# Linear attention and a ResMLP block on one core: two copies of q moved to ScalarE, weight loads moved up in GpSimd's queue, and a new order of all later work

## The chip, the cores and the metric

The kernel runs on one core of a Trainium2 chip. The core has five engines with a queue each: TensorE (PE; its weight loads are shown apart as PEld), VectorE (DVE), ScalarE (ACT), GpSimd (POOL) and SyncE (SP). Each works through its own list in order and waits on semaphores for the others. The metric is the device time of one execution in microseconds (us), lower is better.

## The reference

Attention without a softmax, then a norm, then two residual blocks. The inputs q, k and v are [8, 8, 576, 64] (batch, heads, sequence, width of a head); x is laid out as [8, 576, 512].

```
kv  = einsum('bhsd,bhse->bhde', k, v)
out = einsum('bhsd,bhde->bhse', q, kv)
x   = out / sqrt(mean(out*out, -1) + 1e-6) * g_norm      # per head, then heads side by side
a1  = alpha1 * x + beta1
u   = x + lam * einsum('ts,bsd->btd', w_tok, a1)          # mixes the 576 tokens
a2  = alpha2 * u + beta2
y   = u + lam * (relu(a2 @ w_ch1) @ w_ch2)                # 512 -> 2048 -> 512
```

## The kernel before, in words

One batch is one round of work. Its 576 rows are cut into four chunks of 128 and a tail of 64; the tails of two batches share one tile, so most tail work happens once per two batches. A batch goes through these steps, with the lines that the profile shows:

- Loads: k and v by GpSimd (load_kv, L1395 for 512 rows, L1399 for the tail), q by SyncE (load_q, L1387, four loads a batch). GpSimd also loads both weights of the channel mix in four pieces each (load_w1 L1372, load_w2 L1378). In the trace both are named in_moe_w_ch_dram.
- Attention: kᵀv on PE (L634, tails L640), copied out by ACT (L651) and DVE (L653, tile kvc). q is transposed, for the first two batches on PE (qt_early: copies into a padded tile at L583 or L586, transposes L590, copies out L600 and L603), later by DVE and ACT (L1405, L1408).
- Norm: q·kv on PE (L725), square on ACT (L692), sum on DVE (L695), root on ACT (L698), reciprocal and products on DVE (L701, L703, L710), and the product for the token mix on GpSimd (L713, tile rm; for the tails DVE L708, tile rtl). The first batch has its own form of it (norm_half, L751 to L787).
- Token mix: PE L808, tails L853; the sum is added by DVE (L818). GpSimd turns the result to bf16 (L896) and SyncE transposes it by DMA (L909, tiles a2m, and a2l for the tails).
- Channel mix: first layer on PE (L1020, tails L1034), relu on ACT (L913, tails L1042 or L1051); second layer on PE (L1081) for the first two batches, with the sums added by L1257 and L1266. From the third batch on, the second layer is done by Strassen's scheme with seven products in place of eight: sums of blocks on DVE (L1104), products on PE (L1142), kept sums through ACT (L1172) and GpSimd (L1175), last sums on DVE (L1180). For the last two batches the first layer is done the same way over the pair (L961, evicted by ACT L973 and DVE L983, relu L987 or L913).
- Folds: after the second batch, alpha2 is multiplied into the first weight (fold_w1, L1062, DVE) and lam into the second (fold_w2, L1071).
- The result goes out by SyncE (L1271, L1276, L1193, L1189).

What sets the order: all steps are first recorded as numbered operations with what they read and write. The table ORDER then lists these numbers in the order in which they are issued: each engine's list is that order cut down to its own operations. A number followed by a colon gives the PSUM banks of what it writes, two numbers with a plus are two groups of matmuls woven one by one, and ~n stands for n spare matmuls that keep PE busy (L461). GATES adds a few dependences. Semaphores are worked out from the order afterwards. So an operation that waits holds up everything behind it in its engine's list, and nothing else sets priorities. ORDER's numbers and banks have no meaning by themselves; what they do is shown below as rows of each engine.

The first batches' q copies, with the condition that the change edits:

```
dst, src = qi[b][j][:, :, 64 * m:64 * m + 64], (q0s, q1s)[b][:, at[m]]
if m and not b:
    P.op("ACT", act(576), lambda e, ...: e.activation(dst, src, ACT.Identity), ...)
else:
    P.op("POOL", pool(576, 0), lambda e, ...: e.tensor_copy(out=dst, in_=src), ...)
```

Of the kernel before, what the change touches and what calls it, by code (L numbers as in the profile page):

```python
# [24 lines left out]
13 0 3 6 30 4 31 ~32 14 7 1 32 12 9 28 5 8 207 10 11 27 21 36 35 20 34 29 19 48 42:1 47 ~5 18 26  # L25
16 49:2 25 15 17 2 51:4 55:5:6 50 ~3 56 52 43 23 53:3 44:7 57 61 58 22 62 59 63 54 60 64 126:1 45
72:4:5 37 127 65:2:3 73 41 128 79:6 311 312 74 66 189 136:1:7 24 188 80 67 75 190 76 137 81 68 191
129 69 77 39 82 38 ~2 70 134:5 78 142 130:4 138 135 143 139 132:2 144 83 140 84 131 86:5 87 ~3 145
# [1522 lines left out]
```

## Time and profile before

| what | value |
|---|---|
| median of three runs | 334.18 us (333.53 to 335.07) |
| the profiled execution | 333.56 us |
| its span, first to last instruction | 331.7 us |
| granted TensorE clock | 1.000 |
| matmuls | 2457 |
| PE busy | 321.7 us, 97% |
| DVE busy | 250.8 us, 76% |
| ACT busy | 175.7 us, 53% |
| POOL busy | 150.2 us, 45% |

The span leaves out 1.86 us before the first and behind the last instruction. Times in rows are counted from the span's start. A row of the timeline gives the start, the busy time, the engine, the line, the operation, its output and inputs, and the number of instructions of that kind in a row; in brackets stands how long the engine stood idle before it and what ended that. Matmuls overlap, so the distance between starts says more about PE's pace than the length of one.

### The profile page before, as it was taken

The page shows a single profiled execution, that of the slowest core. Times are in us where ns is not written, and L with a number is a line of the kernel's source. Part 1 is how long each engine was busy: PE and PEld are TensorE (multiplying, and loading weights), DVE is VectorE, ACT ScalarE, POOL GpSimd, SP SyncE. Part 2 cuts the span into 40 slices and gives each one's busy share as a digit, 9 for nine tenths or more (in the row PEclk, how much of TensorE's full clock was granted, in tenths as well). Part 3 has the DMA queues.
Part 4 walks back from the last instruction along what each step waited for, and adds up shares of the span by engine and source line. Part 5 has one row for each costly group of instructions (what it writes and reads, how often), then busy time and mean ns, then how long its engine had stood idle before and what let it go on. Part 6 is the DMA issues. An engine that isn't in the chain of part 4 may idle for free.

```text
span 331.7 us, 6183 instructions
## 1 busy us (share of the span) xinstructions
PE 321.7 (97%) x2457; PEld 218.7 (66%) x2457; DVE 250.8 (76%) x443; ACT 175.7 (53%) x361; POOL 150.2 (45%) x149
## 2 busy tenths in 40 slices
PE   6999899999999999999999999999999999999996
PEld 6777564464676445786579874787568575458884
DVE  3596068669799998939984498769889786989633
ACT  5664573329634482619842676731794059872011
POOL 3599119799253643443357044554325610003432
PEclk9999999999999999999999999999999999999999
DMA  7999999999943996499049942597400170000134
GB/s 243 323 253 230 213 230 201 203 165 275 214 140 79 179 245 116 77 320 192 17 65 268 245 75 50 87 300 163 103 0 3 30 177 0 3 0 2 63 125 130
DMA packets 108532, 48.15 MB, mean 145 GB/s; under 512 B 82061, under 2 KB 101717, under 8 KB 108504
## 3 DMA queue, kind: packets, MB, share of 16 engines
q1 hardware_dynamic: 81520, 26.24, 33.7%
q0 software_dynamic: 26800, 21.38, 33.1%
q8 instruction: 19, 0.31, 0.4%
q10 hardware_dynamic: 184, 0.14, 0.2%
q14 instruction: 9, 0.07, 0.1%
HBM read 38.82 MB, written 9.44 MB: 145 GB/s over the span
## 4 chain that ended last, share of the span: by engine, by line
PE 69%; DVE 14%; POOL 7%; DMA 6%; issue 2%; ACT 2%; SPq 1%; DVEq 0%; POOLq 0%
PE ps L1020 20%; PE ps L1142 18%; PE ps L808 8%; PE ps L961 7%; PE ps L1081 6%; PE ps L1034 3%; DVE small L695 2%; DMA w<-in_moe_w_ch_dram 2%; DVE ps L703 2%; DMA a2l<-a2b 2%; DMA w<-in_k_dram 2%; PE ps L634 2%; DVE xm L710 2%; PE ps L725 2%; POOL rm L713 1%
## 5 line engine op out<-in xcount | busy, mean ns | idle before, releaser
L1020 PE MATMUL ps<-a2m,w 128*128 128x512 bf16 x384 | 98.2, 384 | 1.4 <-DMA w<-in_moe_w_ch_dram 0.8
L713 POOL TENSOR_TENSOR rm<-xm,la_bc 128x512 bf16<-128x512 f32 x28 | 37.2, 1331 | 61.4 <-DVE xm L710 61.2
L1020 PEld LDWEIGHTS ps<-a2m,w 128*128 128x128 bf16 x384 | 36.2, 97 | 39.5 <-issue 1.5
L913 ACT ACTIVATE hh<-ps,b 128x512 bf16<-128x512 f32 x72 | 48.8, 685 | 15.9 <-PE ps L1020 14.8
L1175 POOL TENSOR_TENSOR xm<-xm,tmp 128x512 f32<-128x512 f32 x18 | 25.2, 1411 | 55.1 <-ACT tmp L1172 55.1
L725 PE MATMUL ps<-kvc,qt 128*128 128x128 f32 (+1 forms) x140 | 42.2, 404 | 0.0
L1142 PE MATMUL ps<-w,hh 128*128 128x256 bf16 x344 | 40.5, 273 | 0.1
L1081 PE MATMUL ps<-w,hh 128*128 128x512 bf16 x144 | 37.7, 385 | 0.0
L1142 PEld LDWEIGHTS ps<-w,hh 128*128 128x128 bf16 x344 | 33.5, 98 | 5.9 <-issue 0.4
L634 PE MATMUL ps<-vr,kr 128*128 128x128 f32 x112 | 34.8, 409 | 0.0
L695 DVE TENSOR_REDUCE small<-sq 128x8 f32<-128x512 f32 (+1 forms) x35 | 23.5, 679 | 13.8 <-ACT sq L692 13.4
L1180 DVE TENSOR_TENSOR xm<-ps,xm 128x512 f32<-128x512 f32 x24 | 16.4, 685 | 20.6 <-POOL xm L1175 14.4
L808 PE MATMUL ps<-rm,wt 128*128 128x512 bf16 x112 | 30.2, 382 | 1.0 <-DVE rtl L708 0.4
L1172 ACT ACTIVATE tmp<-ps 128x512 f32<-128x512 f32 (+1 forms) x21 | 11.9, 566 | 33.8 <-PE ps L1142 33.8
L896 POOL CAST a2b<-xm 128x512 bf16<-128x512 f32 x24 | 15.9, 665 | 29.5 <-DVE xm L818 29.4
L692 ACT ACTIVATE sq<-ps 128x512 f32<-128x512 f32 (+1 forms) x35 | 20.6, 595 | 15.9 <-PE ps L725 15.7
L725 PEld LDWEIGHTS ps<-kvc,qt 128*128 128x128 f32 (+1 forms) x140 | 27.2, 195 | 2.1 <-DVE kvc L653 0.8
L703 DVE TENSOR_TENSOR ps<-ps,small 128x512 f32<-128x512 f32 (+1 forms) x35 | 24.2, 693 | 0.5
L913 ACT ACTIVATE hh<-ps 128x512 bf16<-128x512 f32 x32 | 17.6, 597 | 12.4 <-PE ps L1020 12.3
L634 PEld LDWEIGHTS ps<-vr,kr 128*128 128x128 f32 x112 | 22.4, 200 | 1.7
L1081 PEld LDWEIGHTS ps<-w,hh 128*128 128x128 bf16 x144 | 13.3, 97 | 13.6 <-issue 0.4
L1408 ACT ACTIVATE qt<-qp 128x576 fp32r<-128x576 f32 x24 | 16.2, 682 | 8.2 <-DVE qp L1405 8.1
(197 smaller groups left out, 616.8 us busy)
## 6 DMA issues: line engine op xcount, KB each, us to landing
out_dram<-xm SPq DMA_DIRECT2D x32, 256.0 KB, 2.7
kr<-in_k_dram POOLq DMA_DIRECT2D x7, 1024.0 KB, 6.5
vr<-in_v_dram POOLq DMA_DIRECT2D x7, 1024.0 KB, 7.9
qs<-in_q_dram SPq DMA_DIRECT2D x24, 288.0 KB, 4.7
w<-in_moe_w_ch_dram POOLq DMA_DIRECT2D x8, 512.0 KB, 9.9
xm<-in_q_dram SPq DMA_DIRECT2D x8, 288.0 KB, 5.5
qs<-in_v_dram SPq DMA_DIRECT2D x4, 288.0 KB, 6.2
w<-in_k_dram SPq DMA_DIRECT2D x4, 288.0 KB, 6.3
```

Of the source, the lines that this page charges most:

```text
L634: P.mm("fill", 128, [lambda e, t=t, c=c, h=h, o=128 * (h % 4): e.matmul(t.ap()[:, o:o + 128], kr4[:, h, c:c + 2, :].rearrange("p c d -> p ...
L695: P.op("DVE", dve(n), lambda e: e.tensor_reduce(out=st, in_=sq[rs, s3, 0:nst, :], axis=AX.X, op=ALU.add), r=[("sq", s3)], w=[("sm", s4)])
L703: P.op("DVE", dve(n), lambda e: e.tensor_tensor(out=grp(ps()), in0=grp(ps()), in1=st[..., None].to_broadcast([rs.stop - rs.start, nst, DH] ...
L713: P.op("POOL", pool(n), lambda e: e.tensor_tensor(out=r, in0=x.rearrange("p h e -> p (h e)"), in1=la, op=ALU.mult), r=xks + ["la"], w=rks)
L725: P.mm("fill", 128, [lambda e, p=p: e.matmul(dst(p), qt[:, p, cs], kvc[:, i, p, :], start=(p == 0), stop=(p == 3)) for p in range(4)], r=[ ...
L808: P.mm("fill", 512, [lambda e, sc=sc: e.matmul(t.ap(), wt[:, sc if sc < 4 else tw(b), 128 * c:128 * c + 128], rsrc(b, sc, al), start=(sc = ...
L913: P.op("ACT", act(512, 0 if f is None else 1), lambda e: e.activation(dst, t.ap(), ACT.Relu, bias=0.0 if f is None else b1[:, f:f + 1]), r ...
L961: P.mm("main", 512, [lambda e, i=i: e.matmul(t.ap(), lhs[:, i, 128 * x + o:128 * x + o + 128], rhs[:, i, :], start=(first and i == 0), sto ...
L1020: P.mm("main", 512, [lambda e, dj=dj: e.matmul(t.ap(), w1[:, dj, 128 * fj:128 * fj + 128], a2m[:, b % 2, dj, :], start=(dj == 0), stop=(dj ...
L1081: P.mm("main", 512, [lambda e, fj=fj, t=t, c=c: e.matmul(t.ap(), (ht[:, fj, 128 * c:128 * c + 128] if c < 4 else hl[:, fj, :]), w2[:, fj, ...
L1142: P.mm("main", 256, [lambda e, c=c, fj=fj: e.matmul(t.ap()[:, 256 * c:256 * c + 256], at[:, fj, 128 * c:128 * c + 128], rhs(fj), start=(fi ...
L1175: P.op("POOL", pool(256 * n), lambda e, cs=cs, f=f: e.tensor_tensor(out=X[:, cs, f], in0=X[:, cs, f], in1=two(tmp[:, s]), op=ALU.add), r=x ...
```

## The change

The condition in qt_early for the second batch is widened, and the table ORDER is replaced. No operation is added or taken away, the matmuls and the spare ones are the same, and GATES is the same.

```diff
@@ ORDER @@
-13 0 3 6 30 4 31 ~32 14 7 1 32 12 9 28 5 8 207 10 11 27 21 36 35 20 34 29 19 48 42:1 47 ~5 18 26
-16 49:2 25 15 17 2 51:4 55:5:6 50 ~3 56 52 43 23 53:3 44:7 57 61 58 22 62 59 63 54 60 64 126:1 45
...
+47 16 15 17 49:2 2 51:4 50 55:5:6 52 ~3 43 23 56 53:3 22 57 44:7 61 58 62 59 63 60 54 64 45 126:1
+72:4:5 127 65:2:3 37 73 79:6 311 312 74 66 136:1:7 128 41 80 67 75 137 189 24 76 68 81 188 ~2 129
...
@@ qt_early @@
             for m in range(2):
                 dst, src = qi[b][j][:, :, 64 * m:64 * m + 64], (q0s, q1s)[b][:, at[m]]
-                if m and not b:
+                if m == j if b else m:
                     P.op("ACT", act(576), lambda e, dst=dst, src=src: e.activation(
                         dst, src, ACT.Identity), r=[("st", key, at[m])], w=[("qi", b, j, m)])
                 else:
```

For the second batch (b = 1) each of the two steps j has two copies m; the one with m equal to j now runs on ACT at L583, the other stays on GpSimd at L586. PE's list is the same up to about 53 us, so ahead of that only the lists of the other engines differ.

The first place is GpSimd's list at about 22 us, where the second batch's copies of q (qp and xm), its loads of v (vr) and k (kr) and the pieces of the weights (w1, w2) stand. L787 is the first batch's product for the token mix.

```order
-L586 COPY qp<-xm 128x9x64 x2
-L586 COPY xm<-xm 128x9x64
+L586 COPY qp<-xm 128x9x64
 L1395 DMA vr<-in_v_dram 128x8x256
+L1372 DMA w1<-in_moe_w_ch1_dram 128x4x512
 L787 TENSOR_TENSOR rm<-xm,la_bc 128x2x256 x2
 L787 TENSOR_TENSOR rtl<-xt,la_bc 64x256
-L1372 DMA w1<-in_moe_w_ch1_dram 128x4x512 x2
+L1372 DMA w1<-in_moe_w_ch1_dram 128x4x512
```

Two copies have left the list ahead of v's load, and the second piece of w1 stands right behind that load instead of behind three products. Further down, the fourth quarter of w2 moves up behind the third in the same way, from behind the first L713.

The second place is DVE's list at about 213 us, in the Strassen step of the fifth batch. hh and hs are the hidden values and their sums, xm the rows of the result. Before:

```order
L1104 TENSOR_TENSOR hh<-hh 128x4x256
L710 TENSOR_TENSOR xm<-ps,g_bc 128x512
L1104 TENSOR_TENSOR hs<-hh 128x1024
L1180 TENSOR_TENSOR xm<-ps,xm 128x2x256
L1104 TENSOR_TENSOR hh<-hh,hs 128x4x256
L1104 TENSOR_TENSOR hh<-hs,hh 128x4x256
L1104 TENSOR_TENSOR hh<-hh,hs 128x4x256
L1104 TENSOR_TENSOR hh<-hs,hh 128x4x256
L695 TENSOR_REDUCE small<-sq 128x8 x2
```

And after:

```order
L1104 TENSOR_TENSOR hh<-hh 128x4x256
L710 TENSOR_TENSOR xm<-ps,g_bc 128x512
L1104 TENSOR_TENSOR hs<-hh 128x1024
L1104 TENSOR_TENSOR hh<-hs,hh 128x4x256
L1104 TENSOR_TENSOR hh<-hh,hs 128x4x256
L1104 TENSOR_TENSOR hh<-hs,hh 128x4x256
L695 TENSOR_REDUCE small<-sq 64x8
L1104 TENSOR_TENSOR hh<-hh,hs 128x4x256
L695 TENSOR_REDUCE small<-sq 128x8
L701 RECIPROCAL small<-small 64x8
L695 TENSOR_REDUCE small<-sq 128x8
L1180 TENSOR_TENSOR xm<-ps,xm 128x2x256
```

The four sums that read both hh and hs stood behind the L1180 and stand ahead of it now, with a reduction of the seventh batch's norm between them. PE's list at that place changes with them: before, 36 L1034 of the tails (20 and 16, with eight products between) stood ahead of the first product with ab_bc and hh, and now it is 12 L1034 and four L1020, with 12 L1034 behind the products.

The third place is PE's list at about 267 us, where the channel mix of the last two batches begins: w and a2l are the first weight and the tails' input to it.

```order
 L1142 MATMUL ps<-w,hh 128x256 x16
-L1142 MATMUL ps<-ws,hh 128x256 x16
+L1142 MATMUL ps<-ws,hh 128x256 x8
+L1034 MATMUL ps<-a2l,w 128x128 x4
+L1142 MATMUL ps<-ws,hh 128x256 x8
+L1034 MATMUL ps<-a2l,w 128x128 x36
+L961 MATMUL ps<-a2m,w 128x512 x4
 L1034 MATMUL ps<-a2l,w 128x128 x20
-L961 MATMUL ps<-a2m,w 128x512 x4
-L1034 MATMUL ps<-a2l,w 128x128 x24
 L961 MATMUL ps<-qp,qs 128x512 x4
```

Forty L1034 stand ahead of the first L961 where 20 stood before. Behind this, the L961 of the pair stage and the tails still to come are interleaved in another way. At about 55 us PE has 16 L1081 ahead of the token mix of the second batch where it had 12, and 16 behind its tails where it had 20.

More of the change, by code (lines that the diff above doesn't have):

```diff
@@ L24 @@
 ORDER = """
-13 0 3 6 30 4 31 ~32 14 7 1 32 12 9 28 5 8 207 10 11 27 21 36 35 20 34 29 19 48 42:1 47 ~5 18 26
-16 49:2 25 15 17 2 51:4 55:5:6 50 ~3 56 52 43 23 53:3 44:7 57 61 58 22 62 59 63 54 60 64 126:1 45
-72:4:5 37 127 65:2:3 73 41 128 79:6 311 312 74 66 189 136:1:7 24 188 80 67 75 190 76 137 81 68 191
-129 69 77 39 82 38 ~2 70 134:5 78 142 130:4 138 135 143 139 132:2 144 83 140 84 131 86:5 87 ~3 145
[75 rows of a table removed]
+13 3 6 0 4 30 7 14 ~32 31 9 12 1 32 8 28 5 10 207 11 27 21 48 35 20 36 34 19 26 29 18 42:1 25 ~5
+47 16 15 17 49:2 2 51:4 50 55:5:6 52 ~3 43 23 56 53:3 22 57 44:7 61 58 62 59 63 60 54 64 45 126:1
+72:4:5 127 65:2:3 37 73 79:6 311 312 74 66 136:1:7 128 41 80 67 75 137 189 24 76 68 81 188 ~2 129
+69 77 190 82 191 142 70 138 134:5 78 130:4 39 135 143 132:2 139 38 144 83 140 84 131 86:5 87 ~3
[75 rows of a table added]
 """
```

150 rows, old and new, of the table ORDER are left out of this document.

## The prediction

> **What bounds the kernel now.** I read the busy shares first, then the chain that ended last, then what TensorE waited for.
>
> ```profile
> span 331.7 us, 6183 instructions
> PE 321.7 (97%) x2457; PEld 218.7 (66%) x2457; DVE 250.8 (76%) x443; ACT 175.7 (53%) x361; POOL 150.2 (45%) x149
> PE 69%; DVE 14%; POOL 7%; DMA 6%; issue 2%; ACT 2%; SPq 1%; DVEq 0%; POOLq 0%
> ```
>
> TensorE (PE) is busy for 321.7 of 331.7 us, so a new order of the same matmuls can only win from the 10.0 us in which it stands still. The second view lists its waits by what ended them:
>
> ```profile
> PE ps L1020 <- DMA w<-in_moe_w_ch_dram: 0.8, 1, 0.8
> PE ps L1020 <- DVE w L1062: 0.6, 1, 0.6
> PE ps L1142 <- DVE hh L1104: 0.6, 1, 0.6
> PE ps L1034 <- DMA a2l<-a2b: 0.4, 1, 0.4
> PE ps L808 <- DVE rtl L708: 0.4, 1, 0.4
> ```
>
> Each occurs once. Since PE's list is one serial chain, a wait removed there shortens the span by as much, unless a later wait grows. A wait costs more than its idle time, because a matmul's modelled end lies behind the start of the next. I therefore price each by the distance between starts less the usual distance.
>
> **The front: w1's second piece.** POOL's and PE's rows (start, busy us, instruction, and in brackets the idle time and what ended it):
>
> ```profile
> 22.74 0.66 POOL L586 COPY xm<-xm 128x576 f32<-128x576 f32 x1
> 23.35 0.95 POOL L1395 DMA_DIRECT2D vr<-in_v_dram  x1
> 24.32 2.52 POOL L787 TENSOR_TENSOR rm<-xm,la_bc 128x512 bf16<-128x512 f32 x2
> ...
> 27.47 1.56 POOL L1372 DMA_DIRECT2D w<-in_moe_w_ch_dram  x2
> 33.83 0.41 PE L634 MATMUL ps<-vr,kr 128*128 128x128 f32 x1
> 35.08 0.38 PE L1020 MATMUL ps<-a2m,w 128*128 128x512 bf16 x1 [0.84 <-DMA w<-in_moe_w_ch_dram]
> 35.11 0.41 PE L634 MATMUL ps<-vr,kr 128*128 128x128 f32 x1
> 35.36 0.39 PE L1020 MATMUL ps<-a2m,w 128*128 128x512 bf16 x1
> DMA to landing us min/median/max: 7.5/8.6/10.5
> ```
>
> The last line is of L1372's four loads. The piece issued at 27.47 landed 7.5 us later, at 34.97, and L1020 went at 35.08. From an L634 to the next L1020 it is 35.36 − 35.11 = 0.25, so it could have gone at 34.08: 1.00 us is lost. The change takes two copies out ahead of v's load; copies follow each other at 23.35 − 22.74 = 0.61, so v is issued 1.22 earlier, at 22.13, and the piece right behind it at 22.13 + 0.95 = 23.08, which is 4.39 us sooner. If the queue of loads itself were the limit (v's megabyte stands before it in both orders), nothing is gained; if the latency of 7.5 counts, it lands at 30.6 and the whole 1.00 goes. It has to land only 0.9 us sooner for that, a fifth of the lead. I take **0.8**, with bounds 0 and 1.0. The L787s behind it are pushed by one issue (1.56 / 2 = 0.78) and pulled by 1.22, so they come no later. The fourth quarter of w2 moves ahead of an L713 of the second batch: one more issue of 0.78 there, hidden by the L1081 rows that PE runs before the L808 which reads that product (the one that PE met late near 55 us was DVE's, below); were it not hidden it would cost 0.78. So I set it at nothing.
>
> The trace sits on the careful side of a rule here. "DMA: Bandwidth & Descriptors" of the Trainium skill (Anatomy of one DMA) fits a GpSimd load as 2.0 us plus its bytes over 436 GB/s, which for a 512 KB piece gives an estimate of 3.2 us, less than half of the 7.5 seen; by it the wait would go whole, and the sum would be 0.2 larger.
>
> The two copies land on ACT:
>
> ```profile
> 14.92 0.67 ACT L583 ACTIVATE tmp<-xm 128x576 f32<-128x576 f32 x1
> 22.09 0.30 ACT L779 ACTIVATE small<-small,eps 128x8 f32<-128x8 f32 x1
> 25.13 1.51 ACT L603 ACTIVATE qt<-ps 128x512 fp32r<-128x512 f32 x3 [2.74 <-PE ps L590]
> ```
>
> Two times 0.67 is 1.34 us, from 22.39 to 23.73, within the 2.74 us that ACT stood idle: nothing. Without that cover they would cost 1.34.
>
> **Matmuls put ahead of a wait.** In three places the new order has PE do other work while the late operand arrives.
>
> ```profile
> 53.83 1.67 PE L1081 MATMUL ps<-w,hh 128*128 128x512 bf16 x7
> 55.91 1.04 PE L808 MATMUL ps<-rm,wt 128*128 128x512 bf16 x4 [0.40 <-DVE rtl L708]
> 55.16 0.69 DVE L708 TENSOR_TENSOR rtl<-ps,e_bc 64x512 bf16<-64x512 f32 x1
> 259.12 1.04 PE L808 MATMUL ps<-rm,wt 128*128 128x512 bf16 x4 [0.32 <-POOL rm L713]
> 257.79 1.27 POOL L713 TENSOR_TENSOR rm<-xm,la_bc 128x512 bf16<-128x512 f32 x1 [0.51 <-DVE xm L710]
> 269.36 1.03 PE L961 MATMUL ps<-a2m,w 128*128 128x512 bf16 x4
> 270.79 1.40 PE L1034 MATMUL ps<-a2l,w 128*128 128x128 bf16 x22 [0.40 <-DMA a2l<-a2b]
> ```
>
> At 55 us L1081 starts every (1.67 − 0.38) / 6 = 0.215; the last at 55.12, so L808 was due at 55.34 and came at 55.91: 0.57 lost. The change puts four more L1081 (0.86 us) ahead and takes them from behind the tail: **0.57** gained. At 259.12 the wait is 0.32, on a chain DVE L710 to POOL L713; the change takes a DVE sum (L1104, 0.6 or more) from ahead of L710's chain, and puts that L713 ahead of an L1175 add: one such op is longer than the wait, so **0.32** goes. At 270.79 the last token tails wait for their transpose; L1034 was due at 269.36 + 4 × 0.215 = 270.22, so 0.57 is lost, and 20 L1034 of the earlier tails (about 1.1 us at (1.40 − 0.22) / 21 = 0.056) now stand before it: **0.57** gained. A fourth wait of this kind is not in the list above and is not counted.
>
> **The Strassen sums.** At 218 us DVE stood behind one add whose operand POOL had not yet written:
>
> ```profile
> 218.51 0.69 DVE L1180 TENSOR_TENSOR xm<-ps,xm 128x512 f32<-128x512 f32 x1 [3.62 <-POOL xm L1175]
> 220.32 1.75 DVE L1104 TENSOR_TENSOR hh<-hh,hs 128x1024 bf16<-128x1024 bf16 x1
> 218.83 1.06 PE L1034 MATMUL ps<-a2l,w 128*128 128x128 bf16 x16
> 220.46 1.05 PE L1142 MATMUL ps<-ab_bc,hh 128*128 128x256 bf16 x8 [0.57 <-DVE hh L1104]
> 221.57 1.04 PE L1142 MATMUL ps<-w,hh 128*128 128x256 bf16 x8
> 222.74 1.05 PE L1142 MATMUL ps<-ab_bc,hh 128*128 128x256 bf16 x8
> ```
>
> Four L1104 sums stand behind that L1180, and PE's products wait for them. PE's last L1034 began at 219.67, so the product was due at 219.73 and came at 220.46: 0.73. The next L1142 rows run at 0.11 a matmul; eight from 221.57 would hand over at 222.45, and the next row starts at 222.74: 0.29. The change puts all four sums ahead of the L1180, so they can start 3.6 us sooner. Each is about 0.6 long, one of the four was 1.75 beside a POOL add. PE asks for the first one sooner too: 24 tails fewer (24 × 0.056 = 1.34) and four L1020 more (4 × 0.215 = 0.86) stand ahead of it, 0.48 less, so at 219.25. The sums can start at 218.51 − 3.62 = 214.89, and the lead is over 3 us, even if two of them take 1.75. I take **0.9** of the 1.02.
>
> **The fold of w1.**
>
> ```profile
> 113.31 0.94 DVE L1062 TENSOR_SCALAR w<-w,ab 128x2048 bf16<-128x2048 bf16 x1
> 114.31 1.90 PE L1020 MATMUL ps<-a2m,w 128*128 128x512 bf16 x8 [0.58 <-DVE w L1062]
> 85.84 0.69 DVE L695 TENSOR_REDUCE small<-sq 128x8 f32<-128x512 f32 x1 [0.48 <-ACT sq L692]
> 90.00:100.00 10.00, 10.00 (x82) 6.91 (x80) 10.00 (x20) 3.50 (x8) 5.07 (x4) 1.00 0.50 140
> ```
>
> The last row is of the table by stretch: PE busy 10.00 of 10 us, and behind PEld's 6.91, DVE 10.00 too. Before that DVE still stood idle at times, as at 85.84; the four L1062 come at the end of the run. The same ops stand in it after the change, in another order. Bounds are 0 and the idle 0.58; I take **0.2**. This fold runs beside four loads that POOL issues. The rule against a gain is in "SBUF — State Buffer" of the Trainium skill (Who interferes with whom): a tensor_scalar in a two-port mode and GpSimd lock each other out of a shared port pair. POOL still issues those loads at the same place, so by the rule alone the 0.2 would be 0, and the sum 0.2 smaller.
>
> **The sum.** 0.8 + 0.57 + 0.32 + 0.57 + 0.9 + 0.2 = 3.36 us; at the upper bounds 1.0 + 0.57 + 0.32 + 0.57 + 1.02 + 0.58 = 4.06. Against it stand waits of the new order which no row of before can show. It re-sorts DVE's ops from 80 to 114 us, both engines' from 200 to 230, and the pair stage behind 270, and makes SP issue all eight loads of q in a row ahead of one store. The bounds are 0 and what the old order left in the same stretches, 4.06 less the front's 1.0, about 3.1. I take a third, 1.0, because the covers above are longer than the waits they close, so that small shifts do not reopen them. Net **2.4 us**. The profiled execution took 333.56, 1.86 us around its span; minus 2.4 that is 331.2, a span of 329.3. It lies 0.62 below the median of the three runs, so the forecast of a median is 334.18 − 2.4 = **331.8 us**.
>
> **Rivals.** *Nothing new appears* and all waits go, as bounded: 334.18 − 4.06 = 330.1, and a little less with the uncounted fourth wait. For it: the covers are 0.86 to 3.6 us against waits of 0.3 to 1.0. Against it: the old order too left half a dozen waits that a writer of the order would not have wanted.
>
> *The early gain is swallowed.* DVE is full from 86 to 114 us. If its own work sets the pace there, the 0.8 + 0.57 saved before it only make PE wait longer at 114.31: the sum becomes 3.36 − 1.37 − 0.2 = 1.8, less the 1.0, so 333.4, no change that can be told. Against it: DVE's run begins, at 85.84, with a reduction that waits for ACT, and so moves with it.
>
> *The queue of loads decides the front* (its gain 0): 334.18 − 2.36 + 0.8 = 332.6, just within no change. For it: the four loads' latency goes from 7.5 up to 10.5, as in a queue. Against it: the second piece has the least latency of the four, 7.5.
>
> *Slower: the pair stage.* Behind 270 us every L961 bank is emptied by an ACT op and then a DVE op.
>
> ```profile
> 280.00:290.00 10.00, 10.00 (x48) 4.54 (x47) 9.82 (x18) 8.56 (x16) 0.00 (x0) 1.00 0.01 2
> L983 DVE TENSOR_TENSOR xm<-ps,tmp 128x512 bf16<-128x512 f32 x8 | 5.3, 686 | 2.5 <-PE ps L961 2.4
> L973 ACT ACTIVATE sq<-ps,b 128x512 f32<-128x512 f32 x12 | 8.1, 696 | 2.3 <-PE ps L961 2.2
> ```
>
> DVE has 0.18 us of slack in ten and ACT 1.44, and the new order runs the L961 in longer groups with 20 tails (L1034) pushed in among them. L973 runs 24 times there (12 as in the row, 12 more into the other buffer). If PE has to wait for one more L983 (0.69) at a third of these, that is 8 × 0.69 = 5.5: 334.18 − 3.36 + 5.5 = 336.3. It decides the sign from five such waits on (5 × 0.69 = 3.4). For it: the slack. Against it: before, PE was busy all 10.00 us of that stretch, and DVE itself waited 2.4 us for PE in one group, so it keeps up.
>
> **How the numbers follow.** What a measurement can tell from no change is about 0.5%, 1.7 us: 332.5 to 335.9. The forecast, a gain between 1.7 and 3.7 us (330.5 to 332.5), has a chance of 0.47; nothing new, 330.5 and below, 0.12; the swallowed gain 0.18; the queue of loads 0.13; the pair stage 0.10. So faster 0.59, same 0.31, slower 0.10. Eight times in ten: 329.6, beyond which only a gain above all bounds lies, to 334.5; the forecast's own range is 330.5 to 332.5.
>
> **What would show it.** After the change: PE's L1020 on w1's second piece follows its L634 after 0.25 us, with no DMA wait in the list; ACT's gap before its first L603 holds two L583; L808 near 55, 125 and 258 us and L1034 near 268 show no bracket; the four L1104 run before an L1180 that still waits for POOL. The fold's wait stays within 0.75; if it grows to 2 us, the swallowing is right. In the pair stage PE stays at 10.00 of 10; any L961 that waits for L973 or L983 speaks for the slower case. Wrong overall would be new waits of PE above 1 us in all, or a front that gains nothing though its load is issued 4 us sooner.

## The result, and the profile after

The change takes 331.0 us (median of six runs, 330.61 to 332.1) against 333.45 us of the kernel before (six runs, 332.7 to 335.07). The ratio is 0.9928 with a 95% interval of 0.9898 to 0.9957: 2.45 us less. A second measurement, made later, gave medians of 330.9 and 332.92 us and a ratio of 0.9962 (0.9936 to 0.9987). So the gain is about 2 us, between 0.4% and 0.7%, and its sign is sure in both. The forecast was 331.8, a gain of 2.4.

The head of the page of the changed kernel, answering the lines shown of before:

```profile
span 330.3 us, 6148 instructions
...
PE 320.9 (97%) x2427; PEld 219.3 (66%) x2457; DVE 252.1 (76%) x443; ACT 175.5 (53%) x363; POOL 146.4 (44%) x147
...
PE 71%; DVE 14%; ACT 5%; DMA 4%; issue 2%; SPq 2%; POOL 2%; DVEq 0%
```

This execution took 332.1 us, so its span is only 1.4 us shorter than that of before. PE's busy time is 0.8 lower, but 30 matmul records are missing (2427 of 2457; the weight loads are all there), so that row can't be read as less work. The waits of PE say more (us in all, times, longest):

```profile
PE ps L725 <- ACT qt L1408: 1.4, 2, 1.2
PE ps L808 <- DVE rtl L708: 1.1, 1, 1.1
PE ps L461 <- DVE fil L460: 1.1, 1, 1.1
PE ps L612 <- DMA w<-in_k_dram: 0.8, 1, 0.8
...
PE ps L1020 <- DVE xm L1257: 0.2, 1, 0.2
```

Of the five waits that the prediction listed, four are gone (L1020 for the DMA, L1020 for L1062, L1142 for L1104, L1034 for a2l). The fifth, L808 for the rtl of L708, has its old name but another place: it was at 55 us, and is at 257 now, nearly three times as long. New is L725, which waits for a transposed q, and the short one for L1257.

The front, in the timeline of the changed kernel (start, busy us, instruction, and in brackets the idle time and what ended it):

```profile
22.14 0.95 POOL L1395 DMA_DIRECT2D vr<-in_v_dram  x1
23.09 0.76 POOL L1372 DMA_DIRECT2D w<-in_moe_w_ch_dram  x1
24.02 2.52 POOL L787 TENSOR_TENSOR rm<-xm,la_bc 128x512 bf16<-128x512 f32 x2 [0.17 <-DVE xm L782]
...
22.34 0.67 ACT L583 ACTIVATE qp<-xm 128x576 f32<-128x576 f32 x1
22.92 0.67 ACT L583 ACTIVATE xm<-xm 128x576 f32<-128x576 f32 x1
25.12 1.51 ACT L603 ACTIVATE qt<-ps 128x512 fp32r<-128x512 f32 x3 [1.53 <-PE ps L590]
...
33.82 0.41 PE L634 MATMUL ps<-vr,kr 128*128 128x128 f32 x1
34.07 0.39 PE L1020 MATMUL ps<-a2m,w 128*128 128x512 bf16 x1
```

The piece of w1 is issued at 23.09 where 23.08 was forecast, the L787s start 0.30 earlier, the two copies lie in ACT's gap, whose rest is still 1.53 us, and L1020 follows its L634 after 0.25 us.

Further on, PE and then DVE at the places that the prediction priced:

```profile
55.21 0.81 PE L808 MATMUL ps<-rm,wt 128*128 128x512 bf16 x3
...
113.85 1.04 PE L1020 MATMUL ps<-a2m,w 128*128 128x512 bf16 x4
115.04 8.25 PE L1020 MATMUL ps<-a2m,w 128*128 128x512 bf16 x36 [0.15 <-DVE xm L1257]
...
218.20 1.04 PE L1142 MATMUL ps<-ws,hs 128*128 128x256 bf16 x8
219.07 1.91 PE L1142 MATMUL ps<-ab_bc,hh 128*128 128x256 bf16 x16
220.82 3.66 PE L1142 MATMUL ps<-w,hh 128*128 128x256 bf16 x32
...
257.27 0.81 PE L808 MATMUL ps<-rm,wt 128*128 128x512 bf16 x3 [1.13 <-DVE rtl L708]
```

```profile
214.14 1.76 DVE L1104 TENSOR_TENSOR hh<-hs,hh 128x1024 bf16<-128x1024 bf16 x1
216.00 1.58 DVE L1104 TENSOR_TENSOR hh<-hh,hs 128x1024 bf16<-128x1024 bf16 x1
...
220.76 0.67 DVE L1180 TENSOR_TENSOR xm<-ps,xm 128x512 f32<-128x512 f32 x1
...
254.24 0.71 DVE L703 TENSOR_TENSOR ps<-ps,small 64x512 f32<-64x512 f32 x1
254.98 0.69 DVE L1180 TENSOR_TENSOR xm<-ps,xm 128x512 f32<-128x512 f32 x1
255.68 0.69 DVE L710 TENSOR_TENSOR xt<-ps,g_bc 64x512 f32<-64x512 f32 x1
256.30 0.69 DVE L708 TENSOR_TENSOR rtl<-ps,e_bc 64x512 bf16<-64x512 f32 x1
```

The Strassen products run from 218.20 on at their own pace of 0.11 a matmul, with their sums begun at 214.14 (the forecast's earliest was 214.89). At 257 PE stands 1.13 us for an L708 that the new order put behind an L1180 and an L710 which PE does not need yet.

**Where the time went.** To compare two orders stretch by stretch I took points at which both have issued exactly the same set of matmuls, and the start of the same matmul's weight load in both. The first column is the point in before's time. The others give how much earlier than before, against the previous point, a kernel passes it. In the first 18 us every engine's list is the same in all these kernels, and the executions differ by their starting loads, so this part is left out.

| stretch of before, us | the change | again | no front | k loads | L708 | five repairs |
|---|---|---|---|---|---|---|
| 18.32 to 35.94 | 1.01 | 1.00 | 0.32 | 1.01 | 0.89 | 0.98 |
| to 63.05 | 0.57 | 0.57 | 0.57 | 0.56 | 0.56 | 0.57 |
| to 82.75 | -1.56 | 0.07 | 0.07 | 0.07 | -0.38 | -0.46 |
| to 99.36 | -0.07 | -0.73 | -0.74 | -0.18 | -0.28 | -0.07 |
| to 114.31 | 0.52 | 0.51 | 0.53 | 0.53 | 0.51 | 0.53 |
| to 122.74 | -0.42 | -0.42 | -0.42 | -0.42 | -0.42 | -0.19 |
| to 126.41 | 0.28 | 0.28 | 0.28 | 0.28 | 0.28 | 0.28 |
| to 206.54 | -0.15 | -0.15 | -0.15 | -0.15 | -0.15 | 0.04 |
| to 268.64 | 0.79 | 0.81 | 0.80 | 0.79 | 1.87 | 1.98 |
| to 291.43 | 0.51 | 0.51 | 0.52 | 0.52 | 0.52 | 0.52 |
| to 313.30 | 0.00 | 0.00 | -0.01 | 0.00 | 0.00 | 0.00 |

"Again" is a second execution of the same change; the last four columns are experiments told below. Between the first two columns, which are one kernel, only the two rows from 63 to 99 us differ by more than 0.02 us. The column "again" sums to 2.45.

### The profile page after: what moved, and what is told of

It is laid out like the page before. It is cut to its first block, busy times and chain, and to the rows that moved or that the text cites. A ratio compares the mean times of both kernels' runs of the same rounds, so it can differ in the third digit from the quotient of the medians.

```text
span 330.3 us, 6148 instructions
## 1 busy us (share of the span) xinstructions
PE 320.9 (97%) x2427; PEld 219.3 (66%) x2457; DVE 252.1 (76%) x443; ACT 175.5 (53%) x363; POOL 146.4 (44%) x147
## 4 chain that ended last, share of the span: by engine, by line
PE 71%; DVE 14%; ACT 5%; DMA 4%; issue 2%; SPq 2%; POOL 2%; DVEq 0%
PE ps L1142 21%; PE ps L1020 17%; PE ps L808 7%; PE ps L961 7%; PE ps L1081 6%; PE ps L1034 4%; PE ps L725 3%; DMA qs<-in_q_dram 2%; DVE ps L703 2%; POOL a2b L905 2%; DMA w<-in_k_dram 2%; PE ps L634 2%; ACT hh L913 1%; DVE small L695 1%; DVE qp L1405 1%
## 5 line engine op out<-in xcount | busy, mean ns | idle before, releaser
L1020 PE MATMUL ps<-a2m,w 128*128 128x512 bf16 x372 | 96.6, 385 | 0.6 <-DVE xm L1257 0.2
L713 POOL TENSOR_TENSOR rm<-xm,la_bc 128x512 bf16<-128x512 f32 x28 | 36.7, 1314 | 64.0 <-DVE xm L710 63.9
L1020 PEld LDWEIGHTS ps<-a2m,w 128*128 128x128 bf16 x384 | 35.9, 97 | 38.3 <-DVE xm L1257 0.6
L913 ACT ACTIVATE hh<-ps,b 128x512 bf16<-128x512 f32 x72 | 47.7, 685 | 13.1 <-PE ps L1020 9.4
L1175 POOL TENSOR_TENSOR xm<-xm,tmp 128x512 f32<-128x512 f32 x18 | 23.9, 1342 | 54.1 <-ACT tmp L1172 54.1
L725 PE MATMUL ps<-kvc,qt 128*128 128x128 f32 (+1 forms) x140 | 42.1, 404 | 1.4 <-ACT qt L1408 1.4
L1142 PE MATMUL ps<-w,hh 128*128 128x256 bf16 x344 | 40.2, 273 | 0.0
L1142 PEld LDWEIGHTS ps<-w,hh 128*128 128x128 bf16 x344 | 33.5, 98 | 5.4 <-issue 0.4
L1081 PE MATMUL ps<-w,hh 128*128 128x512 bf16 x138 | 36.5, 385 | 0.1
L634 PE MATMUL ps<-vr,kr 128*128 128x128 f32 x112 | 34.6, 410 | 0.0
L1172 ACT ACTIVATE tmp<-ps 128x512 f32<-128x512 f32 (+1 forms) x21 | 11.9, 566 | 38.4 <-PE ps L1142 38.4
L695 DVE TENSOR_REDUCE small<-sq 128x8 f32<-128x512 f32 (+1 forms) x35 | 23.5, 675 | 10.7 <-ACT sq L692 10.5
L808 PE MATMUL ps<-rm,wt 128*128 128x512 bf16 x106 | 29.1, 382 | 1.2 <-DVE rtl L708 1.1
L725 PEld LDWEIGHTS ps<-kvc,qt 128*128 128x128 f32 (+1 forms) x140 | 27.3, 196 | 4.1 <-ACT qt L1408 2.4
L1180 DVE TENSOR_TENSOR xm<-ps,xm 128x512 f32<-128x512 f32 x24 | 16.4, 686 | 15.7 <-PE ps L1142 8.2
L634 PEld LDWEIGHTS ps<-vr,kr 128*128 128x128 f32 x112 | 22.4, 200 | 1.5
L1081 PEld LDWEIGHTS ps<-w,hh 128*128 128x128 bf16 x144 | 13.4, 97 | 13.8 <-issue 0.4
```

Of the source, the lines that this page charges most:

```text
L634: P.mm("fill", 128, [lambda e, t=t, c=c, h=h, o=128 * (h % 4): e.matmul(t.ap()[:, o:o + 128], kr4[:, h, c:c + 2, :].rearrange("p c d -> p ...
L695: P.op("DVE", dve(n), lambda e: e.tensor_reduce(out=st, in_=sq[rs, s3, 0:nst, :], axis=AX.X, op=ALU.add), r=[("sq", s3)], w=[("sm", s4)])
L713: P.op("POOL", pool(n), lambda e: e.tensor_tensor(out=r, in0=x.rearrange("p h e -> p (h e)"), in1=la, op=ALU.mult), r=xks + ["la"], w=rks)
L725: P.mm("fill", 128, [lambda e, p=p: e.matmul(dst(p), qt[:, p, cs], kvc[:, i, p, :], start=(p == 0), stop=(p == 3)) for p in range(4)], r=[ ...
L808: P.mm("fill", 512, [lambda e, sc=sc: e.matmul(t.ap(), wt[:, sc if sc < 4 else tw(b), 128 * c:128 * c + 128], rsrc(b, sc, al), start=(sc = ...
L913: P.op("ACT", act(512, 0 if f is None else 1), lambda e: e.activation(dst, t.ap(), ACT.Relu, bias=0.0 if f is None else b1[:, f:f + 1]), r ...
```

## The experiments

**The change once more.** No edit: is the L725 wait of 1.25 us at 82.7 part of the change?

> The change once more, unaltered. Theory (the 1.25 us for which TensorE waited at 82.7 us came from one late landing of q's fourth load in that execution, 6.86 us where the same order without the front showed 4.70): the load takes 4.5 to 5.8 us here, the wait is 0.2 to 0.5 us, and the span is about 1 us shorter at equal start. Rival (it belongs to the order): 6.5 us or more and a wait above 1.0 again.

Measured: 330.9 us, the profiled execution 330.92 with a span of 329.1. Its waits:

```profile
PE ps L808 <- DVE rtl L708: 0.9, 1, 0.9
...
PE ps L1081 <- DVE w L1071: 0.2, 1, 0.2
PE ps L725 <- ACT qt L1408: 0.2, 1, 0.2
```

What L725 waits for is a q transposed by L1405, and that one waits for its load. The rows of q's load (who waited for it: us, times), first in the first execution and then in this one:

```profile
  DVE qp L1405: 3.0, 1
```

```profile
  DVE qp L1405: 0.6, 1
```

With the same list of instructions, DVE waited 2.4 us longer for a q load in the one than in the other. So the wait of 1.25 us belongs to that execution and not to the order as such. It is most of why that span is 1.4 us shorter than before's and this one 2.6: between 63 and 99 us the first loses 1.63 us and this one 0.66. The L708 wait, the L1257 wait and the rest came back. With q in time, another wait shows at 87 us, L1081 for L1071. The timeline of POOL, DVE and PE there:

```profile
76.66 2.16 POOL L1071 TENSOR_TENSOR w<-w,lam_bc 128x1024 bf16<-128x1024 bf16 x1
79.71 2.16 POOL L1071 TENSOR_TENSOR w<-w,lam_bc 128x1024 bf16<-128x1024 bf16 x1
...
78.93 3.49 DVE L1104 TENSOR_TENSOR ab_bc<-w 128x1024 bf16<-128x1024 bf16 x1
82.35 2.29 DVE L1071 TENSOR_TENSOR w<-w,lam_bc 128x1024 bf16<-128x1024 bf16 x1
...
87.01 0.39 PE L1081 MATMUL ps<-w,hh 128*128 128x512 bf16 x1 [0.24 <-DVE w L1071]
```

This L1104, an operation that elsewhere takes 0.68 us, lasted 3.49, and ended at 82.42, 0.55 us after GpSimd's second L1071 (79.71 + 2.16 = 81.87), although it had begun 0.78 us ahead of that.

**The k loads.** In the change GpSimd issues the loads of k ahead of one of these L1071, which before stood ahead of them. This run puts it back and nothing else:

```diff
 GpSimd
 L1266 TENSOR_TENSOR xm<-xm,tmp 128x512
+L1071 TENSOR_TENSOR w<-w,lam_bc 128x1024
 L1399 DMA kr<-in_k_dram 64x8x64
 L1395 DMA kr<-in_k_dram 128x8x256
 L1399 DMA vr<-in_v_dram 64x8x64
 L1266 TENSOR_TENSOR xm<-xm,tmp 128x512 x2
-L1071 TENSOR_TENSOR w<-w,lam_bc 128x1024
```

> The change with one GpSimd operation moved back ahead of the loads of k for the fourth batch, as it stood before: one half of lam's fold (L1071, 2.15 us), so that these loads go out about 2 us later. Theory (the fourth load of q for the third batch took 6.86 us in place of 4.70 because k's loads run beside it): it lands near 75.5 in place of 77.5, TensorE's wait of 1.25 us for ScalarE's copy of q at 82.7 falls to 0.3 or less, and of that 1.0 to 1.2 us stays to the end. Rival 1 (the landing has another cause): the wait stays above 1 us. Rival 2 (VectorE's full stretch from 85 to 114 us sets the pace): the wait goes but the lead is gone again at 118 us, and the time is that of the change.

Measured: 330.23 us, ratio to before 0.9921 (0.9891 to 0.9951), span 328.0. DVE and GpSimd at the place:

```profile
70.93 2.14 POOL L1071 TENSOR_TENSOR w<-w,lam_bc 128x1024 bf16<-128x1024 bf16 x1
...
78.71 2.53 POOL L1071 TENSOR_TENSOR w<-w,lam_bc 128x1024 bf16<-128x1024 bf16 x1
78.41 0.84 DVE L1104 TENSOR_TENSOR ab_bc<-w 128x1024 bf16<-128x1024 bf16 x1
79.18 3.15 DVE L1071 TENSOR_TENSOR w<-w,lam_bc 128x1024 bf16<-128x1024 bf16 x1
```

The L1104 begins 0.30 us ahead of that L1071 of GpSimd and lasts 0.84 us; the L1071 of DVE behind it grows from 2.29 to 3.15, and the two together end at 82.33 instead of 84.64. The wait of L1081 is gone, and the stretches from 63 to 99 us together lose 0.11, where the three executions with the change's place and q in time lose 0.66 or 0.67. So 0.55 us of the loss was the place of one GpSimd operation, which reached PE by way of DVE. The expectation had another cause, k's loads that slow q's: the execution above speaks against it, with k's loads in the change's place and q in time.

The "SBUF — State Buffer" page of the Trainium skill (Who interferes with whom) says that a DVE instruction with two inputs in SBUF contends with a GpSimd instruction that reads SBUF, and that the order of issue decides which of them is held. The contention agrees with these rows, which give its size: 3.49 against 0.84 us. The part on the order can't be read from them: by the profile's starts the L1104 was ahead in both, by 0.78 us where it was long and by 0.30 where it was short.

**The L708.** This run moves one DVE operation of the change ahead of two that PE needs later:

```diff
 DVE
 L703 TENSOR_TENSOR ps<-ps,small 64x512
-L1180 TENSOR_TENSOR xm<-ps,xm 128x2x256
-L710 TENSOR_TENSOR xt<-ps,g_bc 64x512
-L708 TENSOR_TENSOR rtl<-ps,e_bc 64x512
+L708 TENSOR_TENSOR rtl<-ps,e_bc 64x512
+L1180 TENSOR_TENSOR xm<-ps,xm 128x2x256
+L710 TENSOR_TENSOR xt<-ps,g_bc 64x512
```

> The change with one VectorE operation moved: the tails' product for the last token mix (L708) ahead of a last sum (L1180) and of the product g (L710) that now stand before it. Theory (that order made the wait of 1.13 us at 257 us): the wait falls to 0.2 or less, and the time is 0.9 to 1.1 us less than the change's. Rival (GpSimd's product L713, which ends at 255.6, or a bank that the delayed L1180 holds is late next): at most 0.5 us is won.

Measured: 329.58 us, ratio 0.9893 (0.9853 to 0.9934). The profiled execution was its slowest, 332.01, because it stood for w_tok at the start; the second row shows that the repair itself works:

```profile
18.02 0.27 PE L1287 MATMUL ps<-idb,hh 128*128 128x128 bf16 x2 [1.65 <-DMA hh<-in_moe_w_tok_dram]
...
257.22 0.81 PE L808 MATMUL ps<-rm,wt 128*128 128x512 bf16 x3
```

No bracket is left, and the stretch from 206 to 268 us gains 1.87 instead of 0.79. So the place of L708 cost the change 1.08 us.

**The front alone, and the change without it.** In the first, before gets the two copies on ACT, w1's second piece right behind v and w2's fourth quarter behind its third, and keeps its order otherwise. In the second, the changed kernel gets the old front. GpSimd's list in the first:

```diff
 GpSimd
-L586 COPY qp<-xm 128x9x64 x2
-L586 COPY xm<-xm 128x9x64
+L586 COPY qp<-xm 128x9x64
 L1395 DMA vr<-in_v_dram 128x8x256
+L1372 DMA w<-in_moe_w_ch_dram 128x4x512
 L787 TENSOR_TENSOR rm<-xm,la_bc 128x2x256 x2
 L787 TENSOR_TENSOR rtl<-xt,la_bc 64x256
-L1372 DMA w<-in_moe_w_ch_dram 128x4x512 x2
+L1372 DMA w<-in_moe_w_ch_dram 128x4x512
...
-L1378 DMA w<-in_moe_w_ch_dram 128x4x512 x3
+L1378 DMA w<-in_moe_w_ch_dram 128x4x512 x4
```

> The old order with nothing but the front of the change: two copies on ScalarE, the second piece of w1 right behind v's load, the fourth quarter of w2 behind the third. Theory (a wait taken away pays one to one, and the loss seen near 81 us belongs to rows that the new order put there): w1's second piece lands about 1.5 us sooner or more, TensorE leads the kernel before by 1.0 us from 36 us on and keeps it to the end: about 1.0 us faster than before (0.3%). Rival (q's loads for the third batch land at a fixed time, so that whatever is saved ahead of 81 us is given back there): the lead is gone by 90 us and the time is that of before.

> The change with its front undone: all copies of the second batch back on GpSimd, w1's second piece behind the products, the fourth quarter of w2 behind the first L713. Theory: the wait for w1 is back at 34 us (1.0 us); everything behind it shifts by as much, and the wait near 81 us stays 1.2 us long: 1.0 us slower than the change. Rival (fixed landing of q): the wait near 81 us shrinks from 1.2 to about 0.3 and the time is that of the change within 0.3 us.

Measured for the front alone: 332.27 us, ratio 0.9986 (0.9964 to 1.0008), which by itself does not tell a gain from none. In the trace, measured from the same matmul, it gains 0.98 us on before between 18 and 36 us, carries that undiminished past 114 us and has 0.88 left at the end. Without the front the change took 331.64 us, ratio 0.9967 (0.9942 to 0.9992), and the old wait is back:

```profile
34.40 0.39 PE L1020 MATMUL ps<-a2m,w 128*128 128x512 bf16 x1 [0.53 <-DMA w<-in_moe_w_ch_dram]
```

It is 0.53 us here and was 0.84 before, with GpSimd's old list up to this point. In a third execution with the old list, that of the sum's place told below, there is no wait:

```profile
34.20 0.41 PE L634 MATMUL ps<-vr,kr 128*128 128x128 f32 x1
34.45 0.39 PE L1020 MATMUL ps<-a2m,w 128*128 128x512 bf16 x1
```

There the piece landed 5.5 us after its issue, where it took 7.5 before and 7.2 without the front, and PE gained the same 0.98 us on before up to 36 us as with the new front. In the seven executions with the piece right behind v's load, L1020 never waits for it. So the new place takes away a wait that the old list has in some executions and not in others: set beside the three at hand it is worth 1.0, 0.7 and 0 us.

**The copies back on GpSimd.** Does the gain of the front come from the load's new place or from the copies? The change, with both copies of the second batch on GpSimd again, ahead of v's load, and the piece still right behind that:

```diff
-                if m == j if b else m:
+                if m and not b:
```

> The change with its two copies back on GpSimd, ahead of v's load; the second piece of w1 still stands right behind that load. v and the piece are issued 1.2 us later than in the change, at about 23.3 and 24.3. Theory (the place in the queue does it, the copies add little): the piece lands by 34.0 and the front's gain of 1.0 us at 36 us stays whole, or all but 0.3 of it. Rival (the 1.2 us are needed, since the piece landed 9.6 us after its issue in the change, behind v): a wait of 0.5 us or more is back.

Measured: 331.15 us, ratio 0.9959 (0.9937 to 0.9981), beside 330.9 of the change on the same chip, a difference too small for the timing. In the trace the front gains 0.67 instead of 1.00. L1020 at 34 us has no wait: the piece landed 9.0 us after its issue at 23.85, in time by its place alone. The 0.33 go elsewhere:

```profile
27.19 1.05 PE L831 MATMUL ps<-rm,wt 128*128 128x256 bf16 x8 [0.46 <-POOL rm L787]
```

The load's issue pushes the L787s back, and the copies' removal pulls them forward by more. The edit needs both halves: the place of the load takes the wait away, and the copies pay for it.

**One sum's place in the old order.** The kernel before, with only the L1180 moved behind three of the four L1104:

```diff
 DVE
 L1104 TENSOR_TENSOR hs<-hh 128x1024
-L1180 TENSOR_TENSOR xm<-ps,xm 128x2x256
 L1104 TENSOR_TENSOR hh<-hh,hs 128x4x256
 L1104 TENSOR_TENSOR hh<-hs,hh 128x4x256
 L1104 TENSOR_TENSOR hh<-hh,hs 128x4x256
+L1180 TENSOR_TENSOR xm<-ps,xm 128x2x256
 L1104 TENSOR_TENSOR hh<-hs,hh 128x4x256
```

> The old order with one VectorE operation moved: the last sum L1180 at 218 us, which waits for GpSimd, now behind three of the four L1104 sums instead of ahead of all. Theory (that place alone made the waits of 0.73 and 0.29 us at 220 and 222 us): both go, and 0.7 to 1.0 us is won by 228 us. Rival (the products' other operands or the bank that L1180 frees are late next): 0.3 us or less.

Measured: 332.26 us, ratio 0.9977 (0.9962 to 0.9993). Measured from 206 us on, the trace is 0.29 us ahead of before at 228 us and 0.58 at 231, not 0.9, and 0.18 of that is lost again at 270 us, where L1034 waits for a2l as before. PE and DVE show why:

```profile
220.10 1.05 PE L1142 MATMUL ps<-ab_bc,hh 128*128 128x256 bf16 x8 [0.85 <-DVE xm L1180]
...
219.36 0.68 DVE L1180 TENSOR_TENSOR xm<-ps,xm 128x512 f32<-128x512 f32 x1
```

The sums are in time now, and PE waits instead for the L1180 itself, because the product goes to the PSUM bank that the L1180 reads (bank 2 in ORDER), the cause that the rival named. In the change that product has another bank (4), so it does not depend on the L1180. The move that the prediction priced is worth 0.3 to 0.6 by itself. That the rest came with the new bank, of which the prediction said nothing, is read from the order and was not tried alone.

**Five repairs.** The change with the two repairs above, and three more of the same kind for the losses at 115, 204 and 236 us: an operation of DVE that PE waits for goes ahead of one that it does not.

```diff
 DVE, the three further ones
-L703 TENSOR_TENSOR ps<-ps,small 128x512
 L1257 TENSOR_TENSOR xm<-ps,xm 128x512
+L703 TENSOR_TENSOR ps<-ps,small 128x512
...
-L703 TENSOR_TENSOR ps<-ps,small 128x512
-L701 RECIPROCAL small<-small 128x8
 L1257 TENSOR_TENSOR xt<-ps,xt 128x512
+L703 TENSOR_TENSOR ps<-ps,small 128x512
+L701 RECIPROCAL small<-small 128x8
...
-L818 TENSOR_TENSOR xm<-ps,xm 128x512
-L1405 STREAM_TRANSPOSE qp<-qs 128x576
-L818 TENSOR_TENSOR xm<-ps,xm 128x512
-L1405 STREAM_TRANSPOSE qp<-qs 128x576
+L1405 STREAM_TRANSPOSE qp<-qs 128x576
+L818 TENSOR_TENSOR xm<-ps,xm 128x512
+L1405 STREAM_TRANSPOSE qp<-qs 128x576
+L818 TENSOR_TENSOR xm<-ps,xm 128x512
...
+L653 TENSOR_TENSOR kvc<-ps,kvo 64x4x64 x2
 L1104 TENSOR_TENSOR qs<-w 128x2x512 x2
-L653 TENSOR_TENSOR kvc<-ps,kvo 64x4x64 x2
```

> The change with five repairs, each of one or two operations moved: GpSimd's half fold (L1071) ahead of k's loads at 70 us; the tails' product L708 ahead of L1180 at 255 us; the last two transposes of q (L1405) ahead of an L818 each at 203 us; kvc's two sums (L653) ahead of two weight sums (L1104) at 236 us; two final sums (L1257) ahead of an L703 each at 114 and 118 us. Theory (these places hold the waits that the new order brought or left): 1.1 at 257, 0.4 to 1.5 at 82, 0.3 each at 206, 236 and 115: 2.2 to 3.3 us less than the change. Rival (VectorE is full there, so a repair only moves the wait): only the 1.1 us at 257 is won.

Measured: 328.45 us (327.57 to 329.3), ratio to before 0.9866 (0.9841 to 0.9891), and 2.45 us below the change on the same chip. It beats both kernels. What PE still waits for, and one of these places:

```profile
span 327.2 us, 6177 instructions
...
PE ps L461 <- DVE fil L460: 1.1, 1, 1.1
PE ps L1287 <- ACT qt L603: 0.6, 1, 0.6
PE ps L1142 <- DVE xm L1180: 0.2, 1, 0.2
```

```profile
144.39 1.92 PE L1142 MATMUL ps<-ws,hh 128*128 128x256 bf16 x16 [0.20 <-DVE xm L1180]
```

The two largest stand at 1 and 17 us, ahead of everything that the change touches. The one at 144 us is new, and PE lost 0.37 us by it. Against the change, the repair at 115 us gained 0.23, the one at 236 gained 0.22 and the one at 204 gained 0.44 (in the table its stretch also holds the 0.37). The one at 70 us can't be read here: q came 1.15 us late, which cost 0.46 by 83 us, and the L1104 lasted 2.42 us in spite of GpSimd's repaired order. From 18 us on the two traces differ by 1.73 us; the rest of the 2.45 between the medians has no place in them.

## Why the prediction was right

The net of 2.4 us is what was measured (2.45, and 2.0 in the second measurement), but it is a sum of errors that cancel, and that they cancel is luck. One of its own signs of being wrong came true: PE's new waits come to more than 1 us (1.45 in the table below). And one of its signs of being right failed: L808 near 258 us still has a bracket. By the column "again" of the table, term by term:

| term | predicted | measured |
|---|---|---|
| front, w1's second piece | 0.8 (0 to 1.0) | 1.00 |
| L1081 ahead of L808 at 55 us | 0.57 | 0.57 |
| fold L1062 at 114 us | 0.2 (0 to 0.58) | 0.51 |
| fourth wait, at 125 us | not counted | 0.28 |
| Strassen sums | 0.9 (to 1.02) | 1.31 |
| L808 at 230 us | not counted | 0.29 |
| L808 at 259 us | 0.32 | -0.57 |
| L1034 ahead of a2l at 270 us | 0.57 | 0.51 |
| new waits, by an allowance | -1.0 | -1.45 |

The 1.31 is worked out like this. From PE's first L1034 there to the first L634 behind the products it took 229.25 - 216.84 = 12.41 us before, and 227.51 - 216.67 = 10.84 in the change, where the stretch holds 20 L1034 less and four L1020 more (0.26 us less work at the prediction's 0.056 and 0.215). The L808 behind that L634 followed it after 0.44 us before and after 0.15 in the change, 0.29 less. The term at 259 is the rest of its stretch: 0.81 - 1.31 - 0.29 + 0.22, the last being the loss at 236 that its repair gave back. The new waits are 0.07 - 0.73 between 63 and 99 us, 0.42 at 115, 0.15 at 206 and 0.22 at 236.

**The front.** Right against the profiled execution of before, and there at its upper bound; against an execution of the old list without the wait it would be nothing, which the bound of 0 covers, but from another cause than the queue that the prediction gave for it. The choice between latency and queue was posed too sharply. The piece landed 9.57 us after its issue in the change, at 32.66, where before it took 7.48, to 34.95. The line view of all four pieces of w1 in the change gives

```profile
DMA to landing us min/median/max: 7.7/9.3/10.1
```

against 7.5/8.6/10.5 before; the other three took 0.1 to 0.5 us less, so the higher median is the second piece's alone. Its time goes with its distance from the issue of v's load: 0.95 us behind that it took 9.0 to 9.7 in the seven executions with the new place, 4.1 us behind 7.5 and 7.2, and 5.0 us behind, in the execution without the wait, 5.5. This fits a queue behind v, as that rival said, but not for the whole lead: of the 4.38 us by which it was issued sooner 2.29 were left at its landing, more than the 0.9 that were needed. The two L583 cost nothing in the gap that was named, and without them 0.33 would have been lost at L787, a place where the prediction saw that the two effects offset each other.

**Matmuls put ahead of a wait.** At 55 and 270 us the method (distance between starts, less the usual distance) gave the gain to 0.06. At 259 the sign was wrong. (The prediction took the idle 0.32 there; by its own method, with 16 matmuls from 256.89 at 0.11, the loss was 0.48, and with L708 put back the place gains about that.) The step that failed is the reading of what stood ahead of L710 on DVE and of L713 on GpSimd. Both had moved as it said, but the step looked only at the operand that PE had waited for. The next L808 needs the rtl of L708 on DVE, and the order had moved that one behind an L1180 and an L710. What was late next was not asked, and it cost 1.08, as putting L708 back showed.

**The Strassen sums.** The direction was right, the size was short by 0.4 and the mechanism by half. The sums do start early and no product waits for them. But the move alone, in the old order, leaves a wait of 0.85 us for the bank. The new order changed the bank too, which stands in its table, where I read only the sequence of operations. The gain above the 1.02 of the two priced gaps fits a third one that the prediction did not list: before, the weight load of L1142 at 224.74 waited 0.36 us for ACT's L1172, and in the change those 32 products run on without a gap.

**The fold.** Predicted 0.2 between bounds, it gained nearly all of its 0.58 at 114.31. The last L1062 took 0.94 us beside GpSimd's loads as before, but began at 112.85 instead of 113.31 in an execution that had no lead by then (-0.05 at 99 us), so the gain is DVE's new order. That an early lead is not swallowed there is shown by the front alone, which kept its own. Against the Trainium skill's rule that was weighed at that place ("SBUF — State Buffer", Who interferes with whom), by which POOL's loads would hold the fold back as before and the gain be 0, the measured 0.51 decides. But DVE's new order then met PE at the next bank: the wait for L1257 gave 0.42 back over the next eight microseconds, and the repair of it returned 0.23 of that.

**The new waits.** The allowance of a third of the bound, 1.0, was a guess of size. Measured are 1.45, or 2.5 if the L708 at 259 is counted here. None of them is in the pair stage, the place of the slower rival. The table by stretch of the change there (sum of the stretch, then PE, PEld, DVE, ACT and POOL busy):

```profile
280.00:290.00 10.00, 9.95 (x62) 5.09 (x62) 9.54 (x17) 8.20 (x18) 0.00 (x0) 1.00 0.01 2
```

PE is busy for 9.95 of 10 us, and the lead is the same at 313 as at 291. Nor does an engine have to be faster where they lie: four of the five repairs only change which of two DVE operations goes first, and the fifth moves one operation of GpSimd. But the repaired order also has a new wait, at 144 us; which of the moves brought it was not tried.

**The rivals.** "Nothing new appears" is false: repairing what appeared brought another 2.45 us (1.73 of it in the traces). "The early gain is swallowed" happened at another place and from another cause: 0.66 of it went between 63 and 99 us, of which 0.55 to the place of GpSimd's L1071, while 114 us gained. "The queue decides the front" is out in its strict form, a gain of 0 for a load issued 4 us sooner, but 2.1 of those 4.4 us went into the longer landing.

## What to carry to other kernels

Where an order is static, price a moved operation by what else its engine now does later: for each wait that goes away, find the next operand of the same matmul group and the bank that it writes, and see where their producers stand in the new list. A wait that goes away was read well here as the distance between starts less the usual distance; the waits that will appear can't be read from the trace of before, and here they took more than a third of what the removed ones gave (1.45 of 3.9 us). Compare two orders at points with the same set of work behind them, and in more than one execution, because a single profile held a wait of 1.25 us that the next one did not, and the wait that the front takes away was 0.84, 0.53 and 0 us in three executions of the old list.

## What the runs showed of the hardware

- A subtraction on DVE with both inputs in SBUF (L1104, 0.68 us elsewhere) took 3.49 us beside a GpSimd multiplication of 2.16 us. The same operation was long (1.77 to 3.50 us) in six of the ten profiled executions, and in all six it ended 0.55 or 0.56 us after GpSimd's operation, as if it had run only then; in the other four it took 0.84 to 0.88. The starts do not tell which of the two is held: it took 0.84 us where it began 0.30 us ahead, but 2.96 where it began 0.25 ahead and 3.49 where it began 0.78 ahead.
- The same load in the same list lands at different times: DVE waited 2.4 us longer for one load of q in one execution than in another, w1's second piece took 5.5, 7.2 and 7.5 us in three executions of the old list (shorter the longer v's load had been on its way), and one execution stood 1.65 us for w_tok at its start. Of seven profiled executions of the new order and its variants, three lost 0.4 to 1.6 us between 63 and 83 us. Whether the eight q loads in a row make that likelier than before was not tried.
